# Softmax denominators from GpSimd instead of TensorE, from pair 11 on, with a new order of all instructions

## The chip, the cores and the metric

The kernel runs on one core of a Trainium2 chip. The metric is the device time of one execution in microseconds (us). Three runs of the kernel before gave 612.24, 612.82 and 614.41 us; the median is 612.82 us.

## The reference

Causal attention over 4 batches of 12 heads with 448 tokens and 64 features, and then a two-layer network on the 1,792 tokens, all in float32:

```python
scores = scale * np.matmul(q, k.transpose(0, 1, 3, 2))
scores = np.where(mask, -1000000000.0, scores)
scores = scores - np.max(scores, axis=-1, keepdims=True)
attn = np.exp(scores)
attn = attn / (np.sum(attn, axis=-1, keepdims=True) + 1e-09)
attn_out = np.matmul(attn, v)
x = attn_out.transpose(0, 2, 1, 3).reshape(B * S, H * D)      # 1792 x 768
h = x @ w_in                                                  # 768 x 2048
out = np.maximum(0.01 * h, h) @ w_out                         # 2048 x 768
```

The weights w_in and w_out arrive as float64.

## The kernel before

**Work.** The 48 heads are handled as 24 pairs u = 0 to 23, six pairs to a batch. Scores are computed transposed: keys lie on partitions, queries along the free dimension, so the maximum and the sum of the softmax run over partitions. The keys of a head are cut in four chunks of 128, 128, 128 and 64 keys; by causality chunk c meets only the queries from 128c on, so its columns are 448, 320, 192 and 64. In tile `t` (128 x 2 heads x 1024) the four chunks lie side by side.

For a pair, in order: TensorE transposes k and q (L376), ScalarE copies them out (`kq`, L379), TensorE computes the scores into PSUM tile `S` (L407, mask added by L421). ScalarE copies chunk 0 to `M` (L442), VectorE folds in the other chunks by max (`M<-S,M`, helper line L236), GpSimd takes the maximum over partitions, one instruction for each head (`MR<-M`, `partition_all_reduce`, L450). VectorE subtracts (`t<-S,MR`, L456), which also frees `S` for the next pair, ScalarE takes the exponential (L463), TensorE multiplies with v (`big<-t,v`, L474).

Every second pair, `finish(u)` makes the denominators of pairs u-1 and u. For batches 0 and 1 TensorE sums all four chunks over partitions by a matmul with a tile of ones (`big<-t,ones`, L494). From batch 2 on VectorE first adds the chunks together (three `t<-t` instructions a pair), and TensorE sums chunk 0 alone:

```python
chunks = order[:1] if b >= ADDS else order
pe(0.78 if b >= ADDS else 1.95, sums, ...)                    # L494
act(S + 55, ... T[sr] <- big ...)                             # L506
dma(7, lambda: T[sc], lambda: T[sr][0:97:32, :]...)           # one DMA for four heads
```

Then `sc` gets 1e-9 and the reciprocal `rc` (L509, L510), goes to DRAM (`scr`), is broadcast back (`rb<-scr`, 64 partitions a head, from ScalarE's DMA queue), VectorE multiplies (`rb<-xu,rb`), and `x` is split in two halves of its precision (`xt<-rb` on ScalarE, `xt<-rb,xt` on VectorE).

Meanwhile VectorE and ScalarE turn 16 blocks of w_in from float64 into two tiles each (`stage`, L318, L320, L322; `wl`, L341). Layer 1 is `h<-xt,wh` and `h<-xt,wl` (L548): 18 matmuls for a block of w_in and a batch, 288 a batch. The matmuls of batches 0 and 1 are laid between the attention of later pairs; those of batches 2 and 3 follow. The x of batch 3 takes the buffer of batch 1, so it can be written only after the last layer-1 matmul of batch 1. When attention is done (`switch`), its buffers are closed, w_out is read and converted, and layer 2 runs (L735).

**What sets the order.** Nothing is scheduled by hand at run time. Each step is recorded with an engine, a planned duration and what it reads and writes; `Plan.emit` then plays the engines forward and writes out, for each engine, a fixed order. Among the steps ready it takes the smallest priority: `turn(kind, u)` is u + LATER[kind], and block f of w_in has PIECE[0] + PIECE[1] * f. Where TensorE would idle, `emit` lays in small matmuls on a zero tile (`warmb`, L306), which nobody reads. All DMAs go through one helper line, L230; its queues are SP and ScalarE's.

Of the kernel before, what the change touches and what calls it, by code (L numbers as in the profile page):

```python
# [8 lines left out]
F32 = mybir.dt.float32  # L9
# [11 lines left out]
    "add": 29.11, "load": 31.13, "v": 31.53, "transpose": 32.21, "features": 48.43, "scores": -32.29,  # L21
    "chunk 0": 29.53, "max": -47.1, "all max": -30.16, "subtract": -15.76, "exp": 53.37, "products": 26.02,
    "take products": 72.72, "sums": -33.79, "take sums": -26.22, "spread": 12.66, "invert": -79.89, "store": -38.91,
    "broadcast": 59.38, "divide": -36.6, "x hi": 59.99, "x lo": 21.48,
# [4 lines left out]
PIECE = (410.28, -44.38)  # L29


SAME = 10.69


class Plan:
# [15 lines left out]
    def op(self, eng, us, emit, r=(), w=(), prio=0.0, late=0.0, after=(), take=None, give=None, rows=128, cfg=0):  # L51
# [13 lines left out]
        self.ops.append((eng, us, emit, deps, prio, late, take, give, rows, cfg))  # L65
        return i

    def emit(self, slack, filler):
# [36 lines left out]
        for _ in range(n):  # L105
# [5 lines left out]
            _, us, emit, _, _, late, take, give, rows, cfg = ops[i]  # L111
# [16 lines left out]
            else:  # L128
                end = free[e] = t + us
# [18 lines left out]
def attention_moe_kernel(  # L148
# [160 lines left out]
    def unpack(out_, in_, words, sign, val, R, G, V, prio, first, base, after=()):  # L309
# [9 lines left out]
            (R, base), (G,), prio, 0.5)  # L319
        dve(DM, lambda: nc.vector.scalar_tensor_tensor(  # L320
            out=g(), in0=word(0), scalar=29, in1=g(), op0=ALU.logical_shift_right, op1=ALU.bitwise_or), (R, base), (G,), prio, chain=0.03)
        return dve(DM, lambda: nc.vector.scalar_tensor_tensor(  # L322
            out=v(), in0=v(), scalar=3, in1=g(), op0=ALU.logical_shift_left, op1=ALU.bitwise_or), (G, base), (V,), prio, chain=0.03)

    def weights_in(prio, fs):

        base = ("x", 0)
        for f in fs:
# [13 lines left out]
                (V, ("wh", f), base), (("wl", f),), prio(f))  # L342
# [43 lines left out]
    ADDS = 2  # L386
# [41 lines left out]
    def softmax(u, sl):  # L428
# [54 lines left out]
    def finish(u):  # L483
# [13 lines left out]

        chunks = order[:1] if b >= ADDS else order
        for w in (u - 1, u) if b >= ADDS else ():
            for c in (2, 1, 0):  # L500
# [3 lines left out]
                   (), [("t", w % NTB, e) for e in range(2)], turn("add", u), chain=0.02)  # L504
        pe(0.78 if b >= ADDS else 1.95, sums, ["ones"] + [("t", w % NTB, e) for w in (u - 1, u) for e in range(2)], [key], turn("sums", u), rows=120, cfg=4, take=key)
        act(S + 55, both(new(sr, p1, [128, S], F32, "sr"), lambda: nc.scalar.activation(out=T[sr], in_=bigs(key[1])[:, 0:S], func=ACTF.Copy)),  # L506
            [key], [sr], turn("take sums", u), give=key)
        dma(7, lambda: T[sc], lambda: T[sr][0:97:32, :].rearrange("o (p j) -> o p j", j=16), [sr], [sc], turn("spread", u), 0.68)
        dve(16, lambda: nc.vector.tensor_scalar(out=T[sc], in0=T[sc], scalar1=1e-9, scalar2=None, op0=ALU.add), (), [sc], turn("invert", u))  # L509
# [6 lines left out]
        for w in (u - 1, u):  # L516
# [302 lines left out]
```

## Time and profile before

| what | value |
|---|---|
| median of three runs | 612.82 us |
| the profiled execution | 613.63 us |
| its span, and what lies around it | 611.5 us, 2.13 us |
| TensorE busy | 595.1 us (97%) |
| VectorE busy | 445.6 us (73%) |
| ScalarE busy | 292.2 us (48%) |
| GpSimd busy | 81.9 us (13%), all of it before 265.3 us |
| mean granted clock | 0.997 of full speed |

Busy time is a mean over stages with different limits: attention of the first pairs and conversion of w_in up to some 165 us, attention under layer 1 up to some 299 us, layer 1 alone up to 403.5 us, then layer 2. PE is TensorE, PEld its weight load, DVE is VectorE, ACT ScalarE, POOL GpSimd, SP the engine that issues most DMAs.

### The profile page before, as it was taken

To read this page: it belongs to the slowest core of one execution; us is meant where nothing else is said; L and a number is where in the kernel's file an instruction comes from. 1 tells how busy PE (TensorE), PEld (TensorE's weight loads), DVE (VectorE), ACT (ScalarE), POOL (GpSimd) and SP (SyncE) were. 2 spreads that over 40 slices of the span, in tenths; PEclk is the share of its full clock that TensorE was granted. 3 is DMA by queue.
4 is the path that set the end of the run, shared out by engine and by line. 5 is a ranking of instruction groups with operands and counts; after the bars stand their busy time and mean duration, and the time that the engine had idled before them with its cause. 6 is when DMAs were issued, how large, how long until landed. Compare 5 with 4: busy or idle time off the path is not lost.

```text
span 611.5 us, 10378 instructions
## 1 busy us (share of the span) xinstructions
PE 595.1 (97%) x3864; PEld 514.4 (84%) x3864; DVE 445.6 (73%) x899; ACT 292.2 (48%) x478; POOL 81.9 (13%) x54
## 2 busy tenths in 40 slices
PE   8989899999999999999999999999999999999997
PEld 7655576689767676779999999999999999999997
DVE  4899998989678677551466899778857575767655
ACT  3778677655555645432333555545333233323331
POOL 2544323321124242220000000000000000000000
PEclk9989999999999999999999999999999999999999
DMA  8977976848375432312588864113523333333201
GB/s 197 215 174 137 189 184 185 201 127 255 118 154 136 123 86 54 92 36 89 191 284 270 285 205 133 62 46 104 155 70 120 89 116 109 101 95 94 70 31 39
DMA packets 130465, 82.89 MB, mean 136 GB/s; under 512 B 72560, under 2 KB 128368, under 8 KB 130416
## 3 DMA queue, kind: packets, MB, share of 16 engines
q1 hardware_dynamic: 126576, 76.74, 44.6%
q10 hardware_dynamic: 3840, 5.51, 3.3%
q8 instruction: 30, 0.49, 0.4%
q14 instruction: 19, 0.16, 0.1%
HBM read 61.87 MB, written 20.27 MB: 134 GB/s over the span
## 4 chain that ended last, share of the span: by engine, by line
PE 68%; DVE 15%; POOL 4%; ACT 4%; issue 3%; DMA 3%; SPq 1%; ACTq 0%; POOLq 0%; DVEq 0%
PE h L735 31%; PE h L548 28%; POOL MR L450 4%; PE S L407 4%; DVE t L456 3%; DVE M L236 3%; PE big L474 2%; DVE stage L322 2%; DVE stage L320 1%; DMA stage<-in_moe_w_in_dram 1%; PE big L376 1%; DVE wl L341 1%; DMA rb<-scr 1%; SPq L230 1%; PE big L494 1%
## 5 line engine op out<-in xcount | busy, mean ns | idle before, releaser
L548 PE MATMUL h<-xt,wh 128*128 128x448 f32 x768 | 223.1, 371 | 1.8 <-DVE t L456 1.8
L735 PE MATMUL h<-W,r 128*128 128x384 f32 x882 | 164.0, 334 | 0.1
L548 PEld LDWEIGHTS h<-xt,wh 128*128 128x128 f32 x768 | 141.2, 188 | 17.3 <-issue 4.2
L735 PEld LDWEIGHTS h<-W,r 128*128 128x128 f32 x882 | 153.7, 188 | 0.7 <-DVE r L601 0.4
L548 PE MATMUL h<-xt,wl 128*128 128x448 f32 x384 | 140.9, 367 | 0.0
L450 POOL PARTITION_ALL_REDUCE MR<-M x48 | 81.3, 1740 | 181.3 <-DVE M L236 145.5
L548 PEld LDWEIGHTS h<-xt,wl 128*128 128x128 f32 x384 | 72.1, 188 | 6.8
L600 ACT ACTIVATE r<-v 128x512 fp32r<-128x512 f32 x70 | 41.9, 599 | 71.9 <-DVE v L598 71.8
L456 DVE TENSOR_TENSOR t<-S,MR 128x64 f32<-128x64 f32 x192 | 67.8, 414 | 5.8 <-POOL MR L450 5.7
L236 DVE TENSOR_TENSOR M<-S,M 128x320 f32<-128x320 f32 x144 | 49.1, 354 | 30.3 <-ACT M L442 20.2
L601 DVE TENSOR_TENSOR r<-v,r 128x512 fp32r<-128x512 f32 x70 | 47.3, 690 | 28.3 <-ACT r L600 26.6
L554 ACT ACTIVATE h<-h 128x448 f32<-128x448 f32 x64 | 34.6, 541 | 66.3 <-PE h L548 40.1
L735 PE MATMUL h<-xw,r 128*128 128x384 f32 x294 | 61.9, 334 | 0.0
L463 ACT ACTIVATE t<-t 128x1024 f32<-128x1024 f32 x48 | 50.7, 1056 | 22.7 <-DVE t L456 20.0
L407 PE MATMUL S<-kq 64*128 64x448 f32 (+3 forms) x384 | 53.5, 413 | 3.0 <-DVE t L456 3.0
L735 PEld LDWEIGHTS h<-xw,r 128*128 128x128 f32 x294 | 51.9, 188 | 0.0
L407 PEld LDWEIGHTS S<-kq 64*128 64x128 f32 x384 | 32.7, 191 | 21.7 <-issue 10.8
L598 DVE TENSOR_TENSOR v<-A 128x512 f32<-128x512 f32 (+1 forms) x71 | 47.8, 690 | 0.0
L474 PE MATMUL big<-t,v 128*64 128x448 f32 (+3 forms) x384 | 46.0, 385 | 0.2 <-ACT kq L379 0.2
L474 PEld LDWEIGHTS big<-t,v 128*64 128x64 f32 x384 | 25.3, 137 | 20.8 <-issue 11.8
L442 ACT ACTIVATE M<-S 128x896 f32<-128x896 f32 (+1 forms) x27 | 22.1, 832 | 21.6 <-PE S L421 21.6
L600 ACT ACTIVATE r<-A 128x512 fp32r<-128x512 f32 x28 | 17.7, 632 | 30.8 <-PE h L735 30.7
(84 smaller groups left out, 517.5 us busy)
## 6 DMA issues: line engine op xcount, KB each, us to landing
gd<-h SPq DMA_DIRECT2D x64, 224.0 KB, 3.1
A<-gd SPq DMA_DIRECT2D x28, 512.0 KB, 3.9
stage<-in_moe_w_in_dram SPq DMA_DIRECT2D x16, 768.0 KB, 7.2
A<-in_moe_w_out_dram SPq DMA_DIRECT2D x16, 768.0 KB, 5.7
kraw<-in_k_dram SPq DMA_DIRECT2D x24, 224.0 KB, 5.4
qraw<-in_q_dram SPq DMA_DIRECT2D x24, 224.0 KB, 5.0
rb<-scr ACTq DMA_DIRECT2D x48, 112.0 KB, 3.0
v<-in_v_dram SPq DMA_DIRECT2D x48, 96.0 KB, 2.2
```

The costliest lines, as they stand in the source:

```text
L236: return dve(n, lambda: nc.vector.tensor_tensor(out=out_(), in0=a(), in1=b(), op=op), r, w, prio, **kw)
L407: nc.tensor.matmul(out=T["S", u, bank, e][:, col:col + n], lhsT=T[kq][rows, 128 * c:128 * c + 128], rhs=T[kq][rows, S + qs:2 * S], start=c ...
L450: P.op("Pool", 1.52, lambda e=e: nc.gpsimd.partition_all_reduce(T[mr][:, e], T[m][:, e], 128, ReduceOp.max), [(*m, e)], [(*mr, e)], turn(" ...
L456: i = dve(len(es) * n, lambda c=c, qs=qs, n=n, es=es: nc.vector.tensor_tensor(out=T[t][:, cut(es), at(c):at(c) + n], in0=s(c, es), in1=T[m ...
L463: act(1024 + 55, lambda e=e: nc.scalar.activation(out=T[t][:, e], in_=T[t][:, e], func=ACTF.Exp, scale=scale), (), [(*t, e)], turn("exp", u))
L474: nc.tensor.matmul(out=bigs(key[1])[64 * e:64 * e + 64, qs:S], lhsT=T[vv][:, c, e, :], rhs=T["t", u % NTB][:, e, 512 * bank + col:512 * ba ...
L548: nc.tensor.matmul(out=T[key][:, :S], lhsT=T[w, f, 1][:, 128 * c:128 * c + 128], rhs=T["xt", b][:, x, :], start=(c == 0 and j == 0), stop= ...
L554: lambda key=key, g=g: nc.scalar.activation(out=T[g], in_=T[key][:, :S], func=ACTF.Prelu, alpha=0.01)),
L598: nc.vector.tensor_tensor(out=x(), in0=get(terms[0]), in1=get(terms[1]), op=ALU.add if terms[2] > 0 else ALU.subtract)
L600: act(n, lambda: nc.scalar.activation(out=hi(), in_=x(), func=ACTF.Copy), [*rd, *hold], [(out_cell, "h")], prio)
L601: return dve(n, lambda: nc.vector.tensor_tensor(out=lo(), in0=x(), in1=hi().bitcast(F32), op=ALU.subtract), [*rd, (out_cell, "h")], [out_c ...
L735: nc.tensor.matmul(out=T[key][:, :HO], lhsT=g()[:, jj * 128:jj * 128 + 128], rhs=W[:, w * HO:(w + 1) * HO], start=(e == 0 and jj == 0 and ...
```

## The change

From the eleventh pair on (`ADDS` is now a pair, u >= 11, where it was a batch, b >= 2), so in seven of the twelve calls of `finish`, the matmuls with ones and ScalarE's copy are gone. VectorE adds the chunks as before (now for pairs 10 and 11 too), and GpSimd sums the result over partitions, one `partition_all_reduce` with add for each head, written into the part of `t` that held chunks 1 and 2. The spread into `sc` takes four DMAs in place of one, each from one row of `t`. The planner learns that GpSimd holds VectorE's second way into SBUF for a part of its instruction (`PORT`, 0.78 us of a max and 2.05 us of an add) and marks by `port=-1` the VectorE instructions that need it. All priorities are new.

```diff
 LATER = {
-    "add": 29.11, ..., "scores": -32.29, ..., "subtract": -15.76, ...
+    "add": 22.52, ..., "scores": -92.57, ..., "subtract": 73.98, ..., "sum all": -60.66, ...
 }
+PORT = (0.78, 2.05)
-PIECE = (410.28, -44.38)
+PIECE = (229.08, -27.72)
-SAME = 10.69
+SAME = 6.72
...
-                end = free[e] = t + us
+                wait = max(reads[1] - t - 0.14, 0.0) if port > 0 and reads[0] <= t else 0.0
+                end = free[e] = t + us + wait
+                if port > 0:
+                    taken.append((t, t + wait + port))
+                elif port < 0:
+                    reads = t, end
...
-    ADDS = 2
+    ADDS = 11
...
-        chunks = order[:1] if b >= ADDS else order
-        for w in (u - 1, u) if b >= ADDS else ():
+        chunks = order[:1] if u >= ADDS else order
+        for w in (u - 1, u) if u >= ADDS else ():
...
-                   (), [("t", w % NTB, e) for e in range(2)], turn("add", u), chain=0.02)
-        pe(0.78 if b >= ADDS else 1.95, sums, ...)
-        act(S + 55, ... T[sr] ... )
-        dma(7, lambda: T[sc], lambda: T[sr][0:97:32, :].rearrange("o (p j) -> o p j", j=16), [sr], [sc], turn("spread", u), 0.68)
+                   (), [("t", w % NTB, e) for e in range(2)], turn("add", w), chain=0.02, port=-1)
+        if u >= ADDS:
+            for w in (u - 1, u):
+                t = ("t", w % NTB)
+                for e in range(2):
+                    P.op("Pool", 2.87, lambda t=t, e=e: nc.gpsimd.partition_all_reduce(T[t][:, e, 512:512 + S], T[t][:, e, 512 - S:512], 128, ReduceOp.add),
+                         (), [(*t, e)], turn("sum all", w), port=PORT[1])
+                for e in range(2):
+                    i = 2 * (w - u + 1) + e
+                    dma(7, lambda i=i: T[sc][28 * i:28 * i + 28, :], lambda t=t, e=e: T[t][0:1, e, 512:512 + S].rearrange("o (p j) -> o p j", j=16),
+                        [(*t, e), sc], [(sc, i)], turn("spread", u), 0.68)
+        else:
+            pe(1.95, sums, ...)
+            act(S + 55, ... T[sr] ... )
+            dma(7, lambda: T[sc], lambda: T[sr][0:97:32, :] ...)
```

In the changed kernel the matmuls with v stand on L487, layer 1 on L572, the max over partitions on L463, the new sums on L522, the subtraction on L469, the helper of the adds on L249, the DMAs on L243.

**TensorE at the end of attention.** Before, the last matmuls with v (L474, pair 23), layer-1 matmuls of batch 1, and the last sums (L494):

```order
L474 MATMUL big<-t_103,v_97 64x64 x2
L548 MATMUL h<-xt_1785,wh_1_1685 128x448 x2
L548 MATMUL h<-xt_1785,wl_1_1702 128x448
L548 MATMUL h<-xt_1785,wh_1_1685 128x448 x2
L548 MATMUL h<-xt_1785,wl_1_1702 128x448
L548 MATMUL h<-xt_1785,wh_1_1685 128x448 x2
L548 MATMUL h<-xt_1785,wl_1_1702 128x448
L494 MATMUL big<-t_102,ones 32x448 x2
L494 MATMUL big<-t_103,ones 32x448 x2
```

And now:

```order
L487 MATMUL big<-t_103,v_97 64x448 x2
L487 MATMUL big<-t_103,v_97 64x320 x2
L487 MATMUL big<-t_103,v_97 64x192 x2
L487 MATMUL big<-t_103,v_97 64x64 x2
L572 MATMUL h<-xt_1697,wh_1_1679 128x448 x2
L572 MATMUL h<-xt_1697,wl_1_1686 128x448
L572 MATMUL h<-xt_1697,wh_1_1679 128x448 x2
```

The sums are gone, and the last matmul with v has moved back in the row of layer-1 matmuls: before, 513 of the 576 layer-1 matmuls of batches 0 and 1 had been issued when it came, now 558.

**GpSimd at the end of its program.** Before, only the max (L450), two instructions a pair:

```order
L450 ISA MR_100<-M_99 128x448 x2
L450 ISA MR_100<-M_98 128x448 x2
L450 ISA MR_100<-M_99 128x448 x2
L814 UNCONDITIONAL_BRANCH
L814 ISA
```

Now a pair of sums (L522) behind each pair of max (L463), and two pairs' sums at the end:

```order
L463 ISA MR_100<-M_99 128x448 x2
L522 ISA t_103<-t_103 128x448 x2
L463 ISA MR_100<-M_98 128x448 x2
L522 ISA t_101<-t_101 128x448 x2
L463 ISA MR_100<-M_99 128x448 x2
L522 ISA t_102<-t_102 128x448 x2
L522 ISA t_103<-t_103 128x448 x2
L838 UNCONDITIONAL_BRANCH
```

So the max of a pair now stands behind both sums of the pair two before it.

**VectorE over one pair of batch 2 or 3.** Before, two pairs' adds (`t<-t`) often came together, behind the subtractions (L456):

```order
L456 TENSOR_TENSOR t_101<-S,MR_100 128x192
L456 TENSOR_TENSOR t_101<-S,MR_100 128x320
L236 TENSOR_TENSOR xt_1969<-rb_213,xt_1969 128x448
L236 TENSOR_TENSOR xt_1969<-rb_123,xt_1969 128x448
L236 TENSOR_TENSOR t_102<-t_102 128x2x64
L236 TENSOR_TENSOR t_102<-t_102 128x2x192
L236 TENSOR_TENSOR t_102<-t_102 128x2x320
L236 TENSOR_TENSOR t_103<-t_103 128x2x64
```

Now one pair's adds stand in the midst of the next pair's subtractions (L469), so that GpSimd gets work each pair:

```order
L469 TENSOR_TENSOR t_102<-S,MR_100 128x64
L469 TENSOR_TENSOR t_102<-S,MR_100 128x448
L249 TENSOR_TENSOR t_101<-t_101 128x2x64
L249 TENSOR_TENSOR t_101<-t_101 128x2x192
L249 TENSOR_TENSOR t_101<-t_101 128x2x320
L469 TENSOR_TENSOR t_102<-S,MR_100 128x192
L469 TENSOR_TENSOR t_102<-S,MR_100 128x320
L469 TENSOR_TENSOR t_102<-S,MR_100 128x64
```

The adds have moved ahead of six of the eight subtractions of the pair that follows.

## Rows read from the trace of the kernel before

**Rows 1.** The page: busy time, share of the span and instructions of each engine.

```profile
PE 595.1 (97%) x3864; PEld 514.4 (84%) x3864; DVE 445.6 (73%) x899; ACT 292.2 (48%) x478; POOL 81.9 (13%) x54
```

**Rows 2.** Stretches: busy us (instructions) of each engine, granted clock, DMA share, GB/s.

```profile
core 0: us, PE busy (x) PEld busy (x) DVE busy (x) ACT busy (x) POOL busy (x), PEclk, DMA share, GB/s
105.00:120.00 15.00, 13.52 (x106) 10.43 (x108) 13.76 (x29) 9.20 (x14) 6.99 (x4) 1.00 0.97 225
135.00:150.00 15.00, 15.00 (x76) 13.90 (x75) 14.00 (x19) 8.98 (x13) 1.03 (x1) 1.00 0.83 252
150.00:165.00 15.00, 13.52 (x69) 12.10 (x68) 12.17 (x22) 8.70 (x14) 2.96 (x2) 1.00 0.27 97
165.00:270.00 105.00, 104.39 (x742) 76.22 (x742) 74.16 (x188) 54.07 (x83) 29.16 (x18) 1.00 0.40 105
345.00:390.00 45.00, 45.00 (x220) 40.87 (x219) 42.35 (x77) 26.11 (x54) 0.00 (x0) 1.00 0.50 164
```

**Rows 3.** Timeline, TensorE: sums and matmuls with v; start, us, [idle before].

```profile
117.77 1.93 PE L494 MATMUL big<-t,ones 128*32 128x448 f32 x32 [1.34 <-ACT kq L379]
119.64 1.95 PE L474 MATMUL big<-t,v 128*64 128x448 f32 x16
...
258.16 0.96 PE L494 MATMUL big<-t,ones 128*32 128x448 f32 x8
259.05 1.95 PE L474 MATMUL big<-t,v 128*64 128x448 f32 x16
260.93 0.67 PE L548 MATMUL h<-xt,wh 128*128 128x448 f32 x2
```

**Rows 4.** Small matmuls on the zero tile, over the whole span: duration ns min/median/max.

```profile
L306 PE MATMUL big<-warmb x142: 190/207/261, 1.0 to 236.1; 128*128 128x64 bf16 x142
```

**Rows 5.** Timeline, TensorE: scores of pairs 15, 16, 17 and 23; chain of waits: layer 1.

```profile
167.36 2.11 PE L407 MATMUL S<-kq 64*128 64x448 f32 x16
181.12 2.11 PE L407 MATMUL S<-kq 64*128 64x448 f32 x16
190.43 2.11 PE L407 MATMUL S<-kq 64*128 64x448 f32 x16
255.92 2.11 PE L407 MATMUL S<-kq 64*128 64x448 f32 x16
271.46 129.55 PE h L548 x626
```

**Rows 6.** The lines of GpSimd's max and of VectorE's adds: duration ns min/median/max.

```profile
L450 POOL PARTITION_ALL_REDUCE MR<-M x48: 1604/1682/2392, 11.9 to 262.1; - x48
L236 DVE TENSOR_TENSOR t<-t x36: 282/559/1059, 131.9 to 269.5; 128x128 f32<-128x128 f32 x12, 128x384 f32<-128x384 f32 x12, 128x640 f32<-128x640 f32 x12
```

**Rows 7.** Timeline, GpSimd: both max of pairs 17 and 23 (195.06, 260.56 us).

```profile
195.06 3.19 POOL L450 PARTITION_ALL_REDUCE MR<-M  x2 [6.12 <-ACT xt L233]
260.56 3.19 POOL L450 PARTITION_ALL_REDUCE MR<-M  x2 [7.31 <-DVE M L236]
```

**Rows 8.** Timeline, GpSimd and VectorE around 174 us.

```profile
171.99 3.41 POOL L450 PARTITION_ALL_REDUCE MR<-M  x2 [13.40 <-DVE M L236]
173.86 1.02 DVE L236 TENSOR_TENSOR t<-t 128x128 f32<-128x128 f32 x1
```

**Rows 9.** VectorE's groups by shape, whole span: busy us, mean ns, idle before.

```profile
L236 DVE TENSOR_TENSOR rb<-xu,rb 128x448 f32<-128x448 f32 x24 | 15.0, 628 | 11.4 <-DMA rb<-scr 10.6 <-ACT xu L480 0.8
L236 DVE TENSOR_TENSOR xt<-rb,xt 128x448 fp32r<-128x448 f32 x24 | 14.4, 618 | 14.3 <-ACT xt L233 14.1
L236 DVE TENSOR_TENSOR t<-t 128x640 f32<-128x640 f32 x12 | 9.8, 816 | 0.2
```

**Rows 10.** Timeline from the end of attention: ScalarE, VectorE, SP, TensorE.

```profile
272.15 0.57 SPq L230 DMA_DIRECT2D sc<-sr  x1
273.97 0.18 DVE L509 TENSOR_SCALAR sc<-sc 112x16 f32<-112x16 f32 x1 [3.67 <-DMA sc<-sr]
285.20 1.03 ACT L233 ACTIVATE xt<-rb 128x448 fp32r<-128x448 f32 x2
298.06 1.36 DVE L236 TENSOR_TENSOR xt<-rb,xt 128x448 fp32r<-128x448 f32 x2
299.56 0.81 SPq L230 DMA_DIRECT2D A<-in_moe_w_out_dram  x2
403.55 0.69 PE L735 MATMUL h<-xw,r 128*128 128x384 f32 x3
```

**Rows 11.** DMA issues by line: KB each, median us from issue to landing.

```profile
rb<-scr ACTq DMA_DIRECT2D x48, 112.0 KB, 3.0
...
scr<-rc SPq DMA_DIRECT2D x12, 7.0 KB, 1.9
```

More of the change, by code (lines that the diff above doesn't have):

```diff
@@ L20 @@
 LATER = {
[L21 to L24, printed above, removed]
+    "add": 22.52, "load": -2, "v": 28.31, "transpose": 26.24, "features": 35.26, "scores": -92.57,
+    "chunk 0": 34.2, "max": 1.94, "all max": -78.95, "subtract": 73.98, "exp": -11.46, "products": 21.4,
+    "take products": -3.65, "sum all": -60.66, "sums": -57.34, "take sums": -48.84, "spread": -77.48, "invert": 55.91,
+    "store": 29.75, "broadcast": 75.15, "divide": 115.64, "x hi": 47.53, "x lo": 71.55,
 }
 EARLY = 8
-PIECE = (410.28, -44.38)
-SAME = 10.69
+PORT = (0.78, 2.05)
+PIECE = (229.08, -27.72)
+SAME = 6.72
 class Plan:
@@ L49, in __init__, with op @@
         self.slot = {}
-    def op(self, eng, us, emit, r=(), w=(), prio=0.0, late=0.0, after=(), take=None, give=None, rows=128, cfg=0):
+    def op(self, eng, us, emit, r=(), w=(), prio=0.0, late=0.0, after=(), take=None, give=None, rows=128, cfg=0, port=0.0):
         i = len(self.ops)
@@ L64, in op @@
         deps.discard(i)
-        self.ops.append((eng, us, emit, deps, prio, late, take, give, rows, cfg))
+        self.ops.append((eng, us, emit, deps, prio, late, take, give, rows, cfg, port))
         return i
@@ L84, in emit @@
         split = None
+        taken, reads = [], (0.0, 0.0)
         draws = sum(o[6] is not None and o[6][0] == fill_pool for o in ops)
@@ L88, in at @@
             take = ops[i][6]
+            if ops[i][10] < 0:
+                r = max(ready[i], free["DVE"])
+                for a, b in taken[-2:]:
+                    r = b if a <= r < b else r
+                return r
             if take is None:
@@ L110, in emit @@
             waiting[e].remove(i)
-            _, us, emit, _, _, late, take, give, rows, cfg = ops[i]
+            _, us, emit, _, _, late, take, give, rows, cfg, port = ops[i]
             t = max(t, at(i))
@@ L508, in finish @@
-        dma(7, lambda: T[sc], lambda: T[sr][0:97:32, :].rearrange("o (p j) -> o p j", j=16), [sr], [sc], turn("spread", u), 0.68)
-        dve(16, lambda: nc.vector.tensor_scalar(out=T[sc], in0=T[sc], scalar1=1e-9, scalar2=None, op0=ALU.add), (), [sc], turn("invert", u))
+                   (), [("t", w % NTB, e) for e in range(2)], turn("add", w), chain=0.02, port=-1)
[10 more added lines that the diff above has]
+        else:
+            pe(1.95, sums, ["ones"] + [("t", w % NTB, e) for w in (u - 1, u) for e in range(2)], [key], turn("sums", u), rows=120, cfg=4, take=key)
+            act(S + 55, both(new(sr, p1, [128, S], F32, "sr"), lambda: nc.scalar.activation(out=T[sr], in_=bigs(key[1])[:, 0:S], func=ACTF.Copy)),
+                [key], [sr], turn("take sums", u), give=key)
+            dma(7, lambda: T[sc], lambda: T[sr][0:97:32, :].rearrange("o (p j) -> o p j", j=16), [sr], [sc], turn("spread", u), 0.68)
```

18 lines of the change are left out of this document (8 added, 10 removed).

## The prediction

> **What bounds the kernel now.** I read the page's busy times first: TensorE is busy 97% of the span [rows 1], so nearly everything that it no longer does can shorten the run. A mean over stages can mislead, so the next view was the table of stretches [rows 2]. Three things are to be seen there. From 105 to 165 us VectorE is the fullest engine (about 14 of 15 us until 150), and TensorE idles 1.48 us in two of the stretches. From 165 to 270 us, where the attention of batches 2 and 3 lies under layer 1, TensorE is busy 104.39 of 105 us while VectorE has 30.8 us free and GpSimd 75.8. From 270 us on TensorE only streams; the chain of waits has 626 layer-1 matmuls in one piece there, 129.55 us or 0.207 us each [rows 5]. The granted clock is 1.00 in all these stretches, so no term below rests on it. A microsecond taken from TensorE between 165 and 270 us therefore moves the end by a microsecond, unless what prepares layer 2 holds the end back, or the softmax no longer keeps up.
>
> **The change, part by part.**
>
> *Sums off TensorE.* The full call (pairs 10 and 11) begins at 117.77 and the matmuls with v behind it at 119.64: 1.87 us. A short call begins at 258.16 and the next work at 259.05: 0.89 us, six times [rows 3]. That is 1.87 + 6 x 0.89 = 7.2 us, all in places where TensorE has layer 1 to go on with: **-7.2 us**. ScalarE loses seven copies, off the path; nothing.
>
> *The order.* The blocks of w_in outrank the softmax earlier than before (PIECE), so the layer-1 work that fills the hole comes earlier, and the attention of pairs 13 to 15 later. The gain has a bound: the idle time of the two stretches, 1.48 + 1.48 = 3.0 us, of which 1.34 us is the wait right ahead of the full sums, which go [rows 2, 3]. The other bound is no gain, since VectorE stays the fullest engine there and now also adds the chunks of pairs 10 and 11 (two times 0.28 + 0.56 + 0.82 = 3.3 us; [rows 6, 9]). I take **-1.0 us**, nearer to the wait that is certain to go than to the whole. The small matmuls on the zero tile become 97 where there were 142, 0.2 us each [rows 4]; they fill waits, so they cost nothing either way.
>
> *The sums on GpSimd.* 28 instructions of a form that the trace doesn't have. The nearest row is the max over the same 128 x 448: 1.60 us at least, 1.68 median [rows 6]. The change's plan books 2.87 us for the sum where it books 1.52 for the max; scaled by 1.60/1.52 that is 3.0 us. From below 1.6, then; from above I bound it by the room: max instructions of pairs 17 and 23 begin 195.06 and 260.56 us, so a pair takes 10.9 us, GpSimd works 3.2 of it [rows 7], and two sums of 3.0 leave 1.7 us free. A sum above 3.85 us would not fit at all. Room is also needed for the hand-over: a pair's adds now stand behind two subtractions of the next pair, and the sums wait for them, so I put their start 1 us after the max has ended. So the softmax keeps its pace up to a sum of some (10.9 - 3.2 - 1.0) / 2 = 3.35 us. I take 3.0, which fits.
>
> *VectorE held back.* At 173.86 us an add of 64 columns took 1.02 us where the quickest took 0.28; GpSimd ran its second max then, from some 173.7 to 175.40 [rows 6, 8]. So VectorE lost 0.74 us to the max, and got on at about 174.6, 0.8 us before the max ended. Only instructions with two operands in SBUF suffer: three adds, the multiply and the split, 0.28 + 0.56 + 0.82 + 0.63 + 0.62 = 2.9 us a pair [rows 6, 9], in some three clusters. If GpSimd holds that way for 0.8 us of each max and 2.05 of each sum (the plan's figures), it holds it 5.7 of 10.9 us; a cluster then waits half the time, about 1 us, or 1.6 us a pair. VectorE has 30.8 us free over the ten pairs of 165 to 270 us [rows 2], 3.1 a pair, so it doesn't become the bound. What reaches TensorE is the part that makes a max or a subtraction late. Scores of pairs 15 and 23 begin 167.36 and 255.92 us, 11.07 us a pair; the quickest spacing, from pair 16 to 17, is 9.3 us [rows 5], so the chain has over 1 us of slack. Bounds: nothing, and all 1.6 us in each of 12 pairs, 19 us. I take 0.14 us a pair, **+1.7 us**, near the low end because of that slack.
>
> *DMAs.* The spread is four DMAs for one, 21 more on SP's queue at some 0.6 us each [rows 10], 12.6 us spread over 110. On that queue stand behind a spread the loads of v, k and q and the stores of layer 1; the spread waits for GpSimd. With the sums in time nothing is late, and I cost it at nothing; its cover is that SP has nothing to issue for some microseconds in each pair.
>
> *The tail.* The x of batch 3 is written when layer 1 of batch 1 has ended: first at 285.20, last at 298.06 + 1.36 = 299.4 us, and w_out is asked for at 299.56 [rows 10]. Before, 63 layer-1 matmuls (13.0 us) came behind the last matmul with v, now 18 (3.7 us). From the last matmul with v on, the last x now needs about 1.7 (adds) + 6.0 (two sums) + 1.8 (spread, 272.15 to 273.97) + 0.4 (reciprocal) + 1.9 (store) + 3.0 (broadcast) + four issues of 0.6 + 1.9 (multiply, copy and split) = 19.1 us [rows 9 to 11], and the old chain gives 3.7 + 14.2 = 17.9. VectorE has 2.65 us free from 345 to 390 us [rows 2], which takes up the 1.2; I cost it at nothing, with a bound of 3 us later.
>
> **Sum:** -7.2 - 1.0 + 1.7 = -6.5 us on an execution of 613.63 us (span 611.5 and 2.1 around it): 607.1. That execution was 0.8 above the median of the runs, so the median should come to **606.3 us**.
>
> **The rivals.**
>
> *A, GpSimd sets the pace a little.* A sum of 3.35 to 3.7 us, or hand-overs longer than 1 us, add 2 x (sum - 3.35) a pair: at 3.5 us 12 x 0.3 = 3.6 us more, so 610. For it: GpSimd goes from 28% (29.16 of 105 us, [rows 2]) to some 84% busy in this stage. Against: 1.7 us free by the scaled figure.
>
> *B, slower: GpSimd sets the pace altogether.* The same queue with a sum beyond it: the max of a pair stands behind both sums of the pair two before. Its price is 24 us for each us above 3.35; against a gain of 8.2 it decides from 3.35 + 8.2/24 = 3.7 us on. At 4.2 us it is +20.4, and the time 613.6 - 8.2 + 20.4 = 626 or, from the median, 625. Late sums would also hold SP's queue, and with it layer 1's stores. Only the sum's length speaks for or against it, which no row shows; 3.7 is 2.3 times the max.
>
> *C, slower: GpSimd shuts VectorE out for the whole of each instruction.* Then the 2.9 us of VectorE's two-operand work and GpSimd's 3.2 + 6.0 can't overlap: 12.1 us a pair against 10.9, 1.2 us in each of 12 pairs, 14 us, and the time is 612.8 - 8.2 + 14 = 619. The add at 173.86 speaks against it: it ended at 174.88, before the max did at 175.40 [rows 8]. This is what the Trainium skill states (SBUF — State Buffer, Who interferes with whom): whichever of the two starts first gets the shared pair of ports for the whole instruction, and the other fully blocks. By that rule the time would be 619; the trace disagrees with "the whole instruction" by 0.5 us at least in that one place.
>
> *D, the gain is lost ahead of layer 2.* w_out is asked for at 299.56 us, VectorE is busy 42.35 of 45 us from 345 to 390, and layer 2 starts at 403.55 [rows 2, 10]. If the tail is 3 us late and the conversion has no slack, TensorE stands before layer 2: 606.3 + 3, and with part of A 611 to 612.5.
>
> **How the numbers follow.** About 0.3%, 1.8 us, is what a measurement here can tell from no change: faster is below 611.0, slower above 614.6. The forecast has 0.56 (its own range 603 to 609), A 0.16, D 0.11, B 0.10, C 0.05, and 0.02 is left for what I don't see. Faster takes the forecast, A but a little, and some of D: 0.75. Slower is B and C: 0.15. The rest, 0.10, is no change. The range reaches from the forecast with the whole 3.0 us of idle time and little contention, 602.0, to D and the top of A, 612.5; left out are B, C and some of the edges.
>
> **What would show it.** Right: no matmuls with ones after some 110 us; TensorE still busy over 99% of its time in the second half of attention; the last layer-1 matmul of batch 1 some 7 us earlier than 285 us, and layer 2 starting some 6.5 us earlier than 403.55; sums of about 3.0 us between the max instructions, with free time before each max; adds of up to some 2 us where a sum runs. Wrong: max instructions that wait on GpSimd's own queue and scores over 11.5 us apart (A, B); VectorE near full with adds as long as GpSimd's sums (C); TensorE waiting around 397 us (D). A sum of 3.7 us or more would make the prediction wrong in its sign.

## The result, and the profile after

The changed kernel took 605.98 us (median of four runs, 603.88 to 606.38) beside 612.56 us for the kernel before on the same chip: ratio 0.988, 95% interval 0.985 to 0.991. Forecast were 606.3 us and 602.0 to 612.5. Six more runs of the changed kernel on another chip (first experiment) put the median of all ten at 606.4.

The profiled execution is the shortest of the ten: 603.88 us, span 602.1. The page's busy times, to be held against [rows 1]:

```profile
PE 585.4 (97%) x3739; PEld 511.8 (85%) x3739; DVE 454.4 (75%) x905; ACT 287.0 (48%) x471; POOL 164.9 (27%) x82
```

TensorE lost 9.7 us of work, GpSimd doubled its own, VectorE gained 8.8. Four of the stretches of [rows 2], in the same columns:

```profile
105.00:120.00 15.00, 14.91 (x86) 12.44 (x84) 14.15 (x27) 9.28 (x14) 8.17 (x4) 1.00 0.87 213
135.00:150.00 15.00, 14.40 (x82) 12.10 (x80) 14.28 (x21) 8.07 (x11) 6.93 (x3) 1.00 0.44 147
150.00:165.00 15.00, 14.10 (x99) 10.98 (x100) 13.60 (x33) 8.09 (x15) 10.71 (x6) 1.00 0.35 95
165.00:270.00 105.00, 104.09 (x716) 81.38 (x716) 76.67 (x192) 52.64 (x79) 87.56 (x40) 1.00 0.38 102
```

From 165 to 270 us TensorE stays at 99% although GpSimd works 87.56 us there instead of 29.16. The idle time of the first stretch is gone; that of 135 to 165 us, 1.48 us before, is still 1.50.

GpSimd's timeline shows the hand-over (start, us, line, in brackets the idle time before and who ended it); the last row is the pair of sums at the end of attention:

```profile
187.67 5.73 POOL L522 PARTITION_ALL_REDUCE t<-t  x2 [0.17 <-issue]
194.74 3.19 POOL L463 PARTITION_ALL_REDUCE MR<-M  x2 [1.34 <-ACT xu L493]
...
210.29 5.96 POOL L522 PARTITION_ALL_REDUCE t<-t  x2 [1.09 <-issue]
217.35 3.19 POOL L463 PARTITION_ALL_REDUCE MR<-M  x2 [1.10 <-DVE M L249]
...
272.85 5.73 POOL L522 PARTITION_ALL_REDUCE t<-t  x2 [1.88 <-DVE t L249]
```

Two sums take 5.73 to 5.97 us here. Of the eleven pairs of sums that stand behind a max from 156 us on, six begin 0.17 us after the max and five some 1.1 us after it, and before the ten max from 163 us on GpSimd is idle for 0.8 to 2.2 us, 1.3 in the mean, mostly waiting for VectorE's `M`: the queue has room. The places of [rows 10], from the timelines of ScalarE (first x of batch 3), SP (first load of w_out) and TensorE (layer 2):

```profile
275.26 1.03 ACT L246 ACTIVATE xt<-rb 128x448 fp32r<-128x448 f32 x2
293.33 0.81 SPq L243 DMA_DIRECT2D A<-in_moe_w_out_dram  x2
393.61 0.69 PE L759 MATMUL h<-xw,r 128*128 128x384 f32 x3
```

Layer 1 of batch 1 ends 9.94 us earlier than before, and layer 2 starts 9.94 us earlier: all was won before 276 us and nothing of it lost behind. These two executions differ by more than the medians do; in the changed kernel's second profile (first experiment) both places come 6.82 us earlier than before (285.20 - 278.38 and 403.55 - 396.73). VectorE's groups of [rows 9], same columns:

```profile
L249 DVE TENSOR_TENSOR xt<-rb,xt 128x448 fp32r<-128x448 f32 x24 | 18.3, 771 | 9.2 <-ACT xt L246 8.9
L249 DVE TENSOR_TENSOR rb<-xu,rb 128x448 f32<-128x448 f32 x24 | 16.6, 708 | 10.1 <-DMA rb<-scr 10.1
L249 DVE TENSOR_TENSOR t<-t 128x640 f32<-128x640 f32 x14 | 11.9, 852 | 0.2
```

The split takes 771 ns in the mean instead of 618, the multiply 708 instead of 628, the widest add 852 instead of 816: about 24 x 0.153 + 24 x 0.080 + 14 x 0.036 = 6.1 us of VectorE held back in these three groups. Two instructions of w_in's conversion met a sum as well and took 2.13 and 2.53 us where such take 0.56 and 0.96, 3.1 us more.

### The profile page after: what moved, and what is told of

The parts are those of the page before. It is cut to its first block, busy times and chain, and to the rows that moved or that the text cites. A ratio compares the mean times of both kernels' runs of the same rounds, so it can differ in the third digit from the quotient of the medians.

```text
span 602.1 us, 10229 instructions
## 1 busy us (share of the span) xinstructions
PE 585.4 (97%) x3739; PEld 511.8 (85%) x3739; DVE 454.4 (75%) x905; ACT 287.0 (48%) x471; POOL 164.9 (27%) x82
## 4 chain that ended last, share of the span: by engine, by line
PE 68%; DVE 15%; DMA 5%; ACT 4%; POOL 3%; issue 3%; SPq 1%; ACTq 0%; POOLq 0%; DVEq 0%
PE h L759 31%; PE h L572 28%; DVE t L469 3%; POOL MR L463 3%; PE S L420 3%; PE big L487 3%; DMA stage<-in_moe_w_in_dram 3%; DVE M L249 2%; PE big L389 2%; DVE stage L335 1%; DVE wl L354 1%; DVE stage L333 1%; DVE t L249 1%; DVE stage L331 1%; DMA kraw<-in_k_dram 1%
## 5 line engine op out<-in xcount | busy, mean ns | idle before, releaser
L572 PE MATMUL h<-xt,wh 128*128 128x448 f32 x768 | 223.0, 371 | 0.5 <-DVE t L469 0.5
L572 PEld LDWEIGHTS h<-xt,wh 128*128 128x128 f32 x768 | 141.2, 188 | 13.8 <-PE big L389 0.7
L572 PE MATMUL h<-xt,wl 128*128 128x448 f32 x384 | 140.8, 367 | 0.0
L463 POOL PARTITION_ALL_REDUCE MR<-M x48 | 82.4, 1760 | 97.1 <-DVE M L249 79.7
L522 POOL PARTITION_ALL_REDUCE t<-t x28 | 82.0, 2974 | 16.0 <-DVE t L249 10.7
L572 PEld LDWEIGHTS h<-xt,wl 128*128 128x128 f32 x384 | 72.1, 188 | 6.6
L469 DVE TENSOR_TENSOR t<-S,MR 128x64 f32<-128x64 f32 x192 | 67.8, 414 | 4.3 <-POOL MR L463 4.3
L249 DVE TENSOR_TENSOR M<-S,M 128x320 f32<-128x320 f32 x144 | 49.3, 355 | 25.1 <-ACT M L455 16.0
L420 PE MATMUL S<-kq 64*128 64x192 f32 (+3 forms) x384 | 53.2, 405 | 3.4 <-DVE t L469 3.2
L487 PE MATMUL big<-t,v 128*64 128x448 f32 (+3 forms) x384 | 47.2, 386 | 1.7 <-ACT kq L392 1.2
L487 PEld LDWEIGHTS big<-t,v 128*64 128x64 f32 x384 | 25.9, 136 | 23.1 <-issue 12.0
```

The source lines that it names most:

```text
L249: return dve(n, lambda: nc.vector.tensor_tensor(out=out_(), in0=a(), in1=b(), op=op), r, w, prio, **kw)
L420: nc.tensor.matmul(out=T["S", u, bank, e][:, col:col + n], lhsT=T[kq][rows, 128 * c:128 * c + 128], rhs=T[kq][rows, S + qs:2 * S], start=c ...
L469: i = dve(len(es) * n, lambda c=c, qs=qs, n=n, es=es: nc.vector.tensor_tensor(out=T[t][:, cut(es), at(c):at(c) + n], in0=s(c, es), in1=T[m ...
L487: nc.tensor.matmul(out=bigs(key[1])[64 * e:64 * e + 64, qs:S], lhsT=T[vv][:, c, e, :], rhs=T["t", u % NTB][:, e, 512 * bank + col:512 * ba ...
L522: P.op("Pool", 2.87, lambda t=t, e=e: nc.gpsimd.partition_all_reduce(T[t][:, e, 512:512 + S], T[t][:, e, 512 - S:512], 128, ReduceOp.add), ...
L572: nc.tensor.matmul(out=T[key][:, :S], lhsT=T[w, f, 1][:, 128 * c:128 * c + 128], rhs=T["xt", b][:, x, :], start=(c == 0 and j == 0), stop= ...
```

## The experiments

What was to be told apart: theory T, the change gains by TensorE's lighter load and pays a little for VectorE's waits; rival R, VectorE's waits cost several us and the order gains more than it was given; and how much a microsecond on TensorE is worth. Unless said otherwise an edit is made in the changed kernel.

**The changed kernel once more** (no edit).

> The changed kernel once more, as the base for the other three. Theory T (TensorE is the bound from some 105 us on, and GpSimd's sums lie hidden beside it) and its rivals all expect what was measured: 606 us, 604 to 606.5, 0.988 of the kernel before.

607.21 us (606.29 to 607.59), ratio 0.991 (0.990 to 0.993), 0.7 us above the range that was expected. The profiled run took 606.96 us, 3.08 more than the one above. Of that, 2.60 us are there already when the scores of pair 11 begin, before the first sum on GpSimd, as TensorE's timeline shows; here the changed kernel's first profile,

```profile
101.92 2.11 PE L420 MATMUL S<-kq 64*128 64x448 f32 x16
```

and here this one:

```profile
104.52 2.11 PE L420 MATMUL S<-kq 64*128 64x448 f32 x16
...
278.38 1.03 ACT L246 ACTIVATE xt<-rb 128x448 fp32r<-128x448 f32 x2
```

So much of the spread between executions arises in a stage that the sums don't touch, and profiles are better compared from there on: from pair 11's scores to the first x of batch 3 it is 173.3 and 173.9 us in these two (275.26 - 101.92 and 278.38 - 104.52). The two kernels with fills at the end of this section, the same up to there but for one small matmul, have 173.8 and 174.2. So the mean is 173.8 us, of which TensorE is busy 170.2 and waits 3.0 to 4.0 (3.6 in the mean). This stretch is used below.

**Without the sums.**

```diff
-                    P.op("Pool", 2.87, lambda t=t, e=e: nc.gpsimd.partition_all_reduce(...),
+                    P.op("Pool", 2.87, none,
```

> Leaves out the 28 sums on GpSimd and nothing else: same order, same DMAs; the denominators of pairs 10 to 23 are then read from columns that hold exponentials. Theory T: the sums and their hold on VectorE cost the end almost nothing, so 0 to 1.5 us less than the changed kernel (604.5 to 606). Rival R (the softmax chain through GpSimd sets the pace, the gain comes from the new order): 3 to 8 us less, 598 to 603.

603.95 us, ratio 0.987 (0.984 to 0.989); the changed kernel on the same chip 607.21. So the sums and what they hold up cost 3.3 us (2.5 against the median of all ten runs), above T's range and at the lower end of R's. The stretch from pair 11's scores to batch 3's first x says somewhat less, 2.1 us (173.8 - 171.7). That is time in which TensorE waits (1.7 us here, 3.6 with the sums); its work is the same within 0.2 us. The stretch (in the columns of [rows 2]), and VectorE's groups without the sums:

```profile
102.38:274.11 171.73, 170.00 (x1129) 135.84 (x1129) 130.10 (x298) 91.08 (x136) 44.52 (x26) 1.00 0.46 127
```

```profile
L249 DVE TENSOR_TENSOR xt<-rb,xt 128x448 fp32r<-128x448 f32 x24 | 14.6, 620 | 9.5 <-ACT xt L246 9.3
L249 DVE TENSOR_TENSOR rb<-xu,rb 128x448 f32<-128x448 f32 x24 | 14.4, 617 | 12.4 <-DMA rb<-scr 12.4
```

The split and the multiply lose 24 x (0.151 + 0.091) = 5.8 us to the sums, and w_in's conversion the 3.1 us said above, 8.9 in all; the widest add loses nothing, for its row is the same here, 852 ns: in this order the widest adds are not held by the sums.

**TensorE work back, twice back, and less.** The matmuls with v get chunk 0 once more in every second pair from 11 on, twice more, or, in the third kernel, leave out chunks 1 to 3 in those pairs. The first kernel's edit:

```diff
+            if u >= ADDS and u % 2:
+                for e in range(2):
+                    nc.tensor.matmul(out=bigs(key[1])[64 * e:64 * e + 64, 0:S], lhsT=T[vv][:, 0, e, :],
+                                     rhs=T["t", u % NTB][:, e, 512 - S:512], start=True, stop=True)
```

> Gives TensorE work back in the places from which the change took it: in each of seven odd pairs (11 to 23) chunk 0 of the matmuls with v runs twice, its first result overwritten. In the trace chunk 0 of both heads takes 0.83 us (448 of 1024 columns of 1.90 us), so 7 x 0.83 = 5.8 us. Theory T: a microsecond of TensorE there is a microsecond of the run, +5.8 us (5 to 6.5), 611 to 612.5. Rival R: the matmuls fall into waits, 0 to +2 us, 606 to 608.

> As e3, with two more runs of chunk 0 in each of the seven odd pairs: 7 x 1.6 = 11.2 us of TensorE's work more than the changed kernel. Theory T: +11 us on 607, 617 to 619. If some waits are there to be filled first (e3 came out +1.2 in the median, while its trace has +3.7 us up to the end of layer 1 of batch 1): +6 to +9, 613 to 616. Rival R: under +4.

> The other way: in the seven odd pairs (11 to 23) the product with v leaves out chunks 1 to 3, so TensorE works 7 x about 1.05 = 7.4 us less than in the changed kernel, in the same order. Theory T: TensorE is still the bound after the change, 5 to 7.4 us less, 600 to 602. Rival R: the softmax chain through VectorE and GpSimd is now the bound, 0 to 2 us less, 605 to 607.

Measured: 608.38 us (0.993, 0.991 to 0.995), 611.0 (0.998, 0.996 to 0.999) and 601.06 (0.981, 0.980 to 0.983). Against 606.4 that is +2.0, +4.6 and -5.3. The first two are too little for the work added and lie between T and R; the third is in T's range. One part has nothing to do with attention: the pure layer-1 stream behind it ran faster in the profiled execution of all three, 2.3 us in sum (last section). The stretch from pair 11's scores to batch 3's first x, which ends before that stream, tells it without this. Here are the changed kernel and the three, in the columns of [rows 2], each from its own pair 11's scores to its own first x:

```profile
101.92:275.26 173.34, 170.30 (x1129) 135.98 (x1129) 137.34 (x299) 90.98 (x137) 123.16 (x53) 1.00 0.45 125
103.05:279.86 176.81, 175.08 (x1157) 137.94 (x1157) 136.15 (x297) 91.07 (x135) 123.08 (x53) 1.00 0.44 123
103.88:285.19 181.31, 180.29 (x1185) 139.97 (x1185) 135.46 (x298) 91.68 (x137) 123.28 (x53) 1.00 0.44 120
104.43:273.32 168.89, 163.71 (x1045) 129.93 (x1045) 137.52 (x297) 90.51 (x136) 123.35 (x53) 1.00 0.47 128
```

Against the changed kernel's means (173.8 us, 170.2 busy, 3.6 of waits), all in us:

| kernel | TensorE's work | its waits | stretch | stretch per us of work |
|---|---|---|---|---|
| back | +4.8 | -1.8 (to 1.7) | +3.0 | 0.6 |
| twice back | +10.1 | -2.5 (to 1.0) | +7.5 | 0.75 |
| less | -6.5 | +1.6 (to 5.2) | -4.9 | 0.75 |

So a microsecond of TensorE's work in this stretch is worth 0.6 to 0.75 us, not 1, though TensorE is busy 98% of it. (The medians, with the stream's 2.3 us taken out, give +4.3, +6.9 and -3.0, which is 0.5 to 0.9.) What does not show went into TensorE's waits or came out of them; the layer-1 matmuls and the fills in the stretch are the same ones in all four. Waits can be filled only once: the second helping of work, 5.2 us, moved the end by 4.5.

**The first head's sum issued twice.**

```diff
-   lambda t=t, e=e: nc.gpsimd.partition_all_reduce(...),
+   lambda t=t, e=e: [nc.gpsimd.partition_all_reduce(...) for _ in range(2 - e)],
```

> On GpSimd the sum of the first head of each pair is issued twice: 14 more of 2.95 us. The order is the same. Per pair GpSimd then works 3.2 + 3 x 2.95 = 12.1 us where pairs are 10.9 to 11 us apart, and in the changed kernel it had 1.1 to 2.2 us free ahead of the max. Theory T with the prediction's rule (beyond the room each microsecond shows in full): 12 pairs x about 1.3 us = +15 us, 615 to 626. If GpSimd had no room at all (rival R): 13 x 2.95 = +38 us, 640 or more. If it has much more room than the trace shows: no change, 606.

627.57 us, ratio 1.027 (1.023 to 1.031): 20.4 us more than the changed kernel beside it. GpSimd's timeline, and a row of TensorE's, the scores of pair 16:

```profile
169.92 3.27 POOL L463 PARTITION_ALL_REDUCE MR<-M  x2
173.35 8.93 POOL L522 PARTITION_ALL_REDUCE t<-t  x3 [0.17 <-issue]
182.19 3.27 POOL L463 PARTITION_ALL_REDUCE MR<-M  x2
```

```profile
187.16 2.11 PE L420 MATMUL S<-kq 64*128 64x448 f32 x16 [1.92 <-DVE t L469]
```

At 182.19 the max begins as the third sum ends, with no wait for its data, and the scores behind it wait 1.92 us for the subtraction that the max holds up. This is rival B's mechanism, and the room that the changed kernel has left is under 2.9 us a pair.

**The order alone.** The new priorities, with the sums on TensorE and ScalarE's copy as before.

```diff
-        if u >= ADDS:
-            ... partition_all_reduce and four spreads ...
+        pe(0.78 if u >= ADDS else 1.95, sums, ...)
+        act(S + 55, ... T[sr] ...)
+        dma(7, lambda: T[sc], lambda: T[sr][0:97:32, :] ...)
```

> The changed kernel with the sums of pairs 10 to 23 back on TensorE (VectorE's adds, then chunk 0 times ones, one spread DMA), under the new priorities, which were not made for it. The kernel before had 612.3, the changed one 606 to 607.2. Theory T (the sums on TensorE are worth their 7 x 0.89 = 6.2 us): 612 to 614. Rival O (most of the gain is the new order's): 607 to 609. If both have a part, as e2 and e3 suggest: 609 to 611.

618.85 us, ratio 1.012 (1.009 to 1.014): slower than both, and outside every expectation. TensorE's longest wait for the softmax, and the stretch behind it in the columns of [rows 2]:

```profile
195.65 3.58 PE L420 MATMUL S<-kq 64*128 64x448 f32 x16 [2.43 <-DVE t L469]
```

```profile
195.00:210.00 15.00, 14.33 (x94) 10.16 (x96) 11.80 (x30) 8.70 (x13) 3.19 (x2) 0.89 0.40 89
```

From pair 11's scores to batch 3's first x this kernel takes 186.1 us (290.60 - 104.53), 12.3 more than the changed one: 7 x 0.89 = 6.2 are the sums, 2.2 are more waits of TensorE (5.7 in all), and the rest is the same work done more slowly. Part of that is from 195 to 210 us, where the granted clock is 0.89 (1.2 GHz, the lower of its two levels, for a part of the time): behind the wait of 2.43 us the scores take 3.58 us instead of 2.11.

**GpSimd sums in the old order.** The kernel before's `LATER`, `PIECE` and `SAME`, with "sum all" where "sums" had been.

```diff
-    "add": 22.52, ..., "sum all": -60.66, "sums": -57.34, ...
+    "add": 29.11, ..., "sum all": -33.79, "sums": -33.79, ...
...
-PIECE = (229.08, -27.72)
+PIECE = (410.28, -44.38)
...
-SAME = 6.72
+SAME = 10.69
```

> The sums on GpSimd under the priorities of the kernel before (the key of the new step takes the value of the old sums), the planner still knowing the ports. Theory T: most of the gain stays, 606 to 609. Rival O: it goes, 611 to 615. A third, that the old priorities place adds and sums so that the max waits for GpSimd: above 615, with max instructions that start within 0.2 us of the end of a sum.

631.84 us, ratio 1.033 (1.030 to 1.035), the third of the expectations. GpSimd's timeline, the first load of w_out, and TensorE's timeline at the start of layer 2:

```profile
191.95 12.12 POOL L522 PARTITION_ALL_REDUCE t<-t  x4
203.98 1.94 POOL L463 PARTITION_ALL_REDUCE MR<-M  x1
```

```profile
332.39 0.81 SPq L243 DMA_DIRECT2D A<-in_moe_w_out_dram  x2
```

```profile
416.62 1.37 PE L759 MATMUL h<-xw,r 128*128 128x384 f32 x3 [16.75 <-issue]
```

The second max of a pair stands behind four sums, and w_out is asked for 32.8 us later than before (332.39 - 299.56). TensorE then stands 16.75 us ahead of layer 2, while VectorE is busy for 25.7 of the 26 us from 390 to 416. This fits rival D's mechanism, at a larger delay than D had. Moving the sums without the order is a loss of 19.3 us. With these priorities neither half of the change is worth having alone, so what each brings can't be split into two addends. An order laid out anew for either half alone was not run.

**The planner without the ports.**

```diff
-PORT = (0.78, 2.05)
+PORT = (0.0, 0.0)
```

> The changed kernel, but the planner is told that GpSimd holds VectorE's way for 0 us (PORT = 0, 0), so its order doesn't avoid it; the priorities are those made with it. Theory T (contention is hidden by VectorE's free time): the order is another in places, 606 to 609. Rival C in a mild form (the holds cost the softmax its pace where the order doesn't dodge them): 609 to 615, with adds and splits of 1.5 us and more in the trace.

612.49 us, ratio 1.000 (0.999 to 1.002): the whole gain is gone. The three groups of VectorE:

```profile
L249 DVE TENSOR_TENSOR xt<-rb,xt 128x448 fp32r<-128x448 f32 x24 | 21.4, 919 | 3.1 <-ACT xt L246 3.1
L249 DVE TENSOR_TENSOR rb<-xu,rb 128x448 f32<-128x448 f32 x24 | 17.9, 764 | 18.0 <-DMA rb<-scr 18.0
L249 DVE TENSOR_TENSOR t<-t 128x640 f32<-128x640 f32 x14 | 14.2, 1012 | 0.5
```

VectorE is held 24 x (0.148 + 0.056) + 14 x 0.160 = 7.1 us more in these three groups, and the run is 6.1 us longer than the changed kernel's median. The order as a whole differs, so this is not the price of the holds alone; it is what the order loses when it is laid out without them.

**One sum over both heads.**

```diff
-   nc.gpsimd.partition_all_reduce(T[t][:, e, 512:512 + S], T[t][:, e, 512 - S:512], 128, ReduceOp.add)
+   nc.gpsimd.partition_all_reduce(T[t][:, :, 512:512 + S], T[t][:, :, 512 - S:512], 128, ReduceOp.add) if e == 0 else None
```

> One sum on GpSimd over both heads of a pair (2 x 448 columns), issued where the first head's stood; the planner's order is unchanged. e2 showed that the sums cost 3.3 us. If a sum has a fixed part, the one takes 4 to 5 us where two took 5.73, GpSimd's max waits less, and the run is 1 to 2 us shorter than the changed kernel: 604.5 to 606. If its length goes with the columns alone (5.7 us) or it holds VectorE for longer at a stretch: no change or up to 2 us longer, 606 to 609.

611.86 us, ratio 0.998 (0.997 to 1.000), worse than either expectation. A group of GpSimd's and one of VectorE's:

```profile
L522 POOL PARTITION_ALL_REDUCE t<-t x14 | 77.2, 5512 | 17.2 <-DVE t L249 9.8 <-issue 6.0 <-PE h L572 1.1
...
L249 DVE TENSOR_TENSOR rb<-xu,rb 128x448 f32<-128x448 f32 x24 | 25.6, 1087 | 8.3 <-DMA rb<-scr 8.3
```

GpSimd's work is shorter (77.2 us where two sums a pair took 82.0), and yet 5.5 us are lost. The multiply takes 1,087 ns in the mean where it took 708 (the split less, 651 where it took 771), and from pair 11's scores to batch 3's first x TensorE waits 9.3 us where it waited 3.6. The likely reading is that one long instruction holds VectorE longer at a stretch and that the order, laid out for two short ones, no longer dodges it. Which of TensorE's waits come from these holds is not shown; the first head's sum also ends later, 5.4 us behind its start instead of 2.9.

**Four fills, and fills in their own banks.** Why the layer-1 stream ran faster in some kernels was open, so small matmuls on the zero tile were laid into it: in the first kernel four of 64, 128, 32 and 96 columns ahead of the first blocks of layer 1 of batch 2, into the bank of pair 23's product, of which they overwrite columns 0 to 127 before ScalarE copies it; in the second one of 64 columns there and three in layer 2, each into the bank that the next real matmul starts afresh, so that all is computed. The second kernel's edit:

```diff
                     if c == 0:
                         bank(key)
+                        if (b, f) == (B - 2, 0):
+                            nc.tensor.matmul(out=T[key][:, 0:64], lhsT=warmb, rhs=warmb[:, 0:64], start=True, stop=True)
...
+                        width = {1: 64, 3: 128, 5: 32}.get(i, 0)
+                        if p == 1 and width:
+                            nc.tensor.matmul(out=T[key][:, 0:width], lhsT=warmb, rhs=warmb[:, 0:width], start=True, stop=True)
```

> The long layer-1 stream behind attention runs at 206.7 ns a matmul in the traces of before, of the changed kernel, e2, e4 and e5, and at 202.7 in e3, e7 and e8, all at the same granted clock. Here four matmuls on the zero tile, of 64, 128, 32 and 96 columns, stand ahead of blocks 0 to 3 of layer 1 of batch 2. If the rate is set anew by what interrupts the stream, it changes behind one of them and stays; if the last one leaves it at 202.7, the run is 560 x 4 ns = 2.2 us less 0.5 us for the fills shorter: 604 to 605. If the rate belongs to something else (data, chip, the whole program), nothing changes but the fills: 606.5 to 608.

> The changed kernel's whole computation, with four small matmuls on the zero tile put into banks that the next real matmul starts afresh: 64 columns ahead of layer 1 of batch 2, and 64, 128 and 32 columns in layer 2 (turns 1, 3 and 5). If the long stream of 448-column matmuls keeps whatever spacing it fell into until something interrupts it, the first one turns it from 206.7 to 202.7 ns for 2 x 288 matmuls, 2.3 us: 604 us against the changed kernel's 606.4, ratio about 0.987. If layer 2 (173.3 ns for 384 columns, some 1,176 of them) has two spacings too, one of its fills shows the other: at 170 ns up to 3 us more, 601 to 603. Rival: the turn seen with four fills came from their number or from overwriting the other bank, or differs by chance from run to run; then 606 to 607 and 206.7 ns as before.

604.36 us (0.987, 0.984 to 0.989) and 603.14 us (602.85 to 604.60; 0.985, 0.983 to 0.987). The second computes everything and is the fastest full version measured, 3.3 us under the changed kernel's median of ten. Layer 2 kept its spacing, so its three fills did nothing there; the first fill's work is shown in the last section.

## Why the prediction was right

The total was right, 606.3 forecast and 605.98 (606.4 over ten runs) measured. The main mechanism was right too: the run is shorter because TensorE has less to do. From the start to batch 3's first x, before and now (columns of [rows 2]):

```profile
0.00:285.20 285.20, 272.20 (x2116) 203.34 (x2117) 217.15 (x521) 163.33 (x241) 81.88 (x54) 0.99 0.59 145
0.00:275.26 275.26, 262.48 (x1991) 200.73 (x1992) 224.19 (x525) 158.31 (x235) 161.57 (x81) 1.00 0.60 150
```

TensorE's work falls by 9.7 us (8.3 in the second profile, 263.93) and its waits stay near where they were, 13.0 us before, 12.8 and 14.5 now. But the addends were not as forecast: errors of both signs met, and that they cancelled so well is luck.

*Sums off TensorE, -7.2.* The work went as said: the last matmul with ones begins at 94.4 us in the changed kernel. But the term was taken too small, for it counted one short call of 0.89 us six times. Three of the six took longer in the kernel before; from the start of each to the next work it is 1.58, 1.26 and 1.74 us:

```profile
176.09 1.65 PE L494 MATMUL big<-t,ones 128*32 128x448 f32 x8
214.90 1.32 PE L494 MATMUL big<-t,ones 128*32 128x448 f32 x8
239.83 1.81 PE L494 MATMUL big<-t,ones 128*32 128x448 f32 x8
```

That makes 1.87 + 3 x 0.89 + 1.58 + 1.26 + 1.74 = 9.1 us. The other way round, the sentence "a microsecond taken from TensorE between 165 and 270 us therefore moves the end by a microsecond" was too strong for the changed kernel, where work added or removed moved the end of the stretch by 0.6 to 0.75 us per us. By that price 9.1 us are worth 5.5 to 6.8 us, an estimate; at the kernel before's own operating point it was not measured. The rest goes into TensorE's waits (3.6 us of them became 5.2 where 6.5 of work were taken away). The likely reading, which no run shows directly, is that in these places the softmax's loop of matmul, VectorE, GpSimd and ScalarE sets the pace; that TensorE is busy 98 or 99% hides it.

*The order, -1.0, with bounds nothing and -3.0.* The term was put on the wrong thing, the idle time of two stretches. One of these went, the other stayed as it was. (VectorE is not the fullest engine there throughout: from 135 to 150 us [rows 2] have 15.00 for TensorE and 14.00 for VectorE.) What the order does is to keep the sums from being waited for and VectorE from being held: laid out without knowledge of the ports the gain is zero (612.49), in the old order the sums cost 19.3 us (631.84). No addend for it can be given, since order and sums only work together.

*The sums' length, 3.0 us.* 5.73 us for two, so 2.87 (2.95 at most as a rule; a few run to 3.43). The hand-over took 0.17 us in six pairs and some 1.1 in five, 0.6 in the mean where 1.0 was taken, so there was more room than the forecast had, and rivals **A** and **B** did not come. The doubled sum showed that B's mechanism is real once the queue is full: 2.87 us more a pair gave 20.4 us. B's price, 24 us for each us by which both sums are longer, is 12 us for each us a pair, here 34 us, less the room that is left; with the measured 1.3 us of room (in the mean) it gives 12 x 1.5 = 18 us.

*VectorE held back, +1.7, with bounds 0 and 19.* Mis-sized twice over, in opposite directions. The holds came to 6.1 us in the three groups above and 3.1 in w_in's conversion, not 1.6 us in each of 12 pairs, in part because the order dodges them (7.1 us more without its knowledge of the ports). But of what was left, a quarter to over a third reached the end (2.1 us by the stretch, 2.5 to 3.3 by the medians, for 8.9 us held by the sums), where 0.14 of 1.6 had been taken. The slack that this leaned on, the difference between the quickest and the mean spacing of scores, covered less than was reckoned. That 1.7 lies near the measured 2.1 to 3.3 is luck. Nor do "only instructions with two operands in SBUF suffer": one of the two in w_in's conversion reads a single operand in SBUF. It takes 0.56 us in the same place without the sums; here it met one that began at 119.30 us:

```profile
119.61 2.13 DVE L331 TENSOR_SCALAR stage<-stage 128x768 int32<-128x768 int32 x1
```

Rival **C**, VectorE shut out for the whole instruction, did not come true. VectorE's timeline of the changed kernel has the longest hold of all:

```profile
275.86 2.28 DVE L249 TENSOR_TENSOR xt<-rb,xt 128x448 fp32r<-128x448 f32 x1 [3.27 <-ACT xt L246]
```

GpSimd's second sum ran until 272.85 + 5.73 = 278.58 us, and began 2.95 us earlier, at 275.6. The split ended at 278.14, 0.44 us before it, and having some 0.6 us of its own to do it got on 1.9 us after the sum began. (The profile's spans of GpSimd are rough; but the same 1.9 us comes out for all nine VectorE instructions of this kernel that a sum held by more than 0.3 us.) The rule of the Trainium skill (SBUF — State Buffer, Who interferes with whom), that the first of the two keeps the ports for its whole instruction, is again too strong by this row, as by [rows 8]; that a sum shuts VectorE out for most of its length, 1.9 of 2.95 us, is what this row shows, and the kernel with ports unknown shows what an order that takes no account of it costs, 6.1 us.

*The tail and rival D.* w_out was asked for 18.1 us after batch 3's first x (293.33 - 275.26) where it had been 14.4: 3.7 us later, above the bound of 3. Costing it at nothing held even so: from that x to layer 2 it is 393.61 - 275.26 = 118.35 us, and before it was 403.55 - 285.20 = 118.35. The conversion had that much slack. In the old order, with w_out asked for 43.7 us after that x (332.39 - 288.73), it had not, and D came.

## What to carry to other kernels

An engine that is busy 98 or 99% need not be the only pace-maker, and a few microseconds of work added or removed go in part into what waits it has: measure what a microsecond of it is worth by adding and removing some, before moving work away from it. A price read from one call of several needs a look at the others. Where one engine's instruction shuts another out of memory, what counts is where the order puts the two; two short instructions that an order was laid out to dodge may beat one long one with less work. A change of work and the order laid out for it should be judged together, and a forecast whose total is right should still be tested by its addends.

## What the runs showed of the hardware that was not expected

A long row of 448-column layer-1 matmuls runs at one of two spacings with the granted clock at 1.00 in both, and keeps the one it has until something interrupts it; in every trace of this case the row behind attention has one spacing from its first tens of matmuls to its end or to a fill. The chain of waits (start, us, number of matmuls) of the changed kernel:

```profile
270.82 120.25 PE h L572 x581
```

That is 207.0 ns each, as before (129.55/626 = 206.9, [rows 5]), and the same 120.25 us for 581 in its second profile. The kernel with fills in their own banks, chain and TensorE's timeline around its first fill:

```profile
277.31 115.45 PE h L574 x570
```

```profile
273.80 0.37 PE L574 MATMUL h<-xt,wl 128*128 128x448 f32 x1
...
276.89 0.37 PE L574 MATMUL h<-xt,wl 128*128 128x448 f32 x1
277.10 0.20 PE L572 MATMUL h<-warmb 128*128 128x64 bf16 x1
...
277.62 0.36 PE L574 MATMUL h<-xt,wl 128*128 128x448 f32 x1
...
280.66 0.36 PE L574 MATMUL h<-xt,wl 128*128 128x448 f32 x1
```

The 15 matmuls ahead of the fill take 3.09 us (206.0 ns each, 276.89 - 273.80), the 15 behind it 3.04 (202.7, 280.66 - 277.62); over 570 of them it is 202.5 ns each, 4.4 ns less. From batch 3's first x to layer 2 the changed kernel takes 118.35 us and this one 393.95 - 277.79 = 116.2. One 64-column matmul of 0.2 us thus gives back some 2 us. The kernels with TensorE work added or removed, the one with ports unknown and the one in the old order fell into the quick spacing by themselves (117.95/581 = 203.0 in two of them); what decides between the two, and why 384-column layer-2 matmuls show only one (173.6 ns with or without fills, 189.24/1090 in the changed kernel and 58.33/336 here), stays open.
